# Attention keys in blocks of 128, with the last 64 of two pairs multiplied with v in the four quarters of the array

## The chip, the cores and the metric

The kernel runs on one core of one Trainium2 chip. The metric is the time on the device in microseconds, from the profiler and from repeated runs; lower is better.

## What is computed

Attention with a sigmoid in place of softmax, for 8 batches, 12 heads, 448 positions and 64 columns a head, and behind it a feed-forward layer over the 3584 tokens:

```python
scores = scale * np.matmul(q, k.transpose(0, 1, 3, 2)) - np.log(S)
attn = 1.0 / (1.0 + np.exp(-scores))
x = np.matmul(attn, v)                 # to (8 * 448, 768)
h = x @ w_in                           # (768, 2048)
g = np.maximum(0.01 * h, h)
return g @ w_out                       # (2048, 768)
```

All of it is float32.

## The kernel before

**Attention.** Two heads make a pair (48 pairs, 6 per batch): the first head's 64 columns lie in partitions 0 to 63, the second's in 64 to 127. The 448 keys are cut into NK = 4 blocks of KR = 112. For one block c, `Pair.scores` takes six matmuls into the PSUM tile `sc`, three for each head (q and k are split into a high and a low part, `qks`, and three of the four products of parts are taken), each with 64 rows, 112 weight columns and 448 streamed columns. The two heads use the two halves of the array's rows. ScalarE then writes sigmoid(scale * scores - log 448) into a tile `s` (pool `at`, five tiles). `Pair.attn_v` multiplies, for each block and head, v of that block (112 rows, 64 columns, fp32, in the halves of the array's columns) with `s`, and sums the four blocks in the PSUM tile `pv`. One slot later `Pair.keep` copies `pv` with ScalarE into a third of the tile `x`, which holds three pairs.

**FFN.** Both matmuls of the layer are taken as seven products of sums of sub-blocks (Strassen's way, in the form of Winograd) in the order `ORDER = 0, 1, 4, 5, 3, 6, 2`. Two batches (q) have four `x` tiles; `Operands` forms their sums and splits them into `so`; `PLAN` and `PLAN_ALONE` say in which slot each such step is given out: "p16": "h002" is the high part of operand 0 in the slot of product 16. `First.step` takes one product of one of NU = 8 units: nine matmuls into PSUM. A `Quad` keeps the results of a unit: product 0, 4, 3 and 2 add into one bank (`px`), product 1 and then 5 and 6 use another (`py`, `pz`). One slot after a product `Quad.done` evacuates it: 0, 4, 5 and 2 with a ScalarE copy, 1, 3 and 6 with a VectorE addition to a copy taken earlier (all of these are `c_h`).

**Order.** All instructions are kept in program order on their engines. The work is given out in slots: `slot` first issues the chores that are due and then the slot's TensorE work. For q = 0 the attention of 12 pairs runs alone. For q = 1 to 3 each pair has four attention slots (scores of blocks 0 and 1 of pair i, `attn_v` of pair i - 1 in two slots, scores of blocks 2 and 3 of pair i), followed by 5, 5 or 4 FFN products of the two batches before. The FFN of the last two batches and the second matmul come behind.

**PSUM.** In q = 0 (`ps_a`): three score tiles of two banks and two `pv`. In q = 1 to 3 (`ps_b`): two score tiles of two banks, one `pv`, two `px`, one `pz`:

```python
psum = banks("ps_b", dict(s=(2, 2), pv=(1, 1), px=(2, 1), pz=(1, 1)))
```

Beside this VectorE takes apart the weights, which come as 64-bit numbers, into float32 (`wr`, `wd`, `ws`, written to `t`), and the weights of each unit are read back and split (`wx`, `w`).

Of the kernel before, what the change touches and what calls it, by code (L numbers as in the profile page):

```python
# [9 lines left out]
F32 = mybir.dt.float32  # L10
F32R = mybir.dt.float32r
I32 = mybir.dt.int32
AF = mybir.ActivationFunctionType
# [3 lines left out]
P = 128  # L17
# [7 lines left out]
ST = 10  # L25
# [6 lines left out]
PRODUCTS = 5, 5, 4  # L32


def _f32(bits):
    return struct.unpack("<f", struct.pack("<I", bits))[0]

W_LEAST = _f32(0x38000000)  # L40
W_MOST = _f32(0x47EFFE00)


@with_exitstack
def attn_ffn_kernel(ctx: ExitStack, tc: tile.TileContext, qk, v, w_in, w_out, out):
# [6 lines left out]

    nc = tc.nc
    B = 8
    S = qk.shape[3]
    NP = qk.shape[0] // B
    D = P // 2
    KR = v.shape[1]  # L60
    NK = S // KR
    NC = out.shape[0]
    NU = w_in.shape[0]
    HW = NC // 2 * P
# [2 lines left out]
    scale = 1.0 / math.sqrt(D)  # L67
    bias = -math.log(S)
    heads = [slice(j * D, j * D + D) for j in range(2)]
# [4 lines left out]
    def pinned(issue):  # L74

        return lambda *args, **kw: tc.keep_in_program_order(issue(*args, **kw))  # L76

    mm, dma = pinned(nc.tensor.matmul), pinned(nc.sync.dma_start)
    copy, act = pinned(nc.scalar.copy), pinned(nc.scalar.activation)
# [14 lines left out]
    def later(slots, *fns, first=False):  # L94

        chores.setdefault(now + slots, ([], []))[not first].extend(fns)
# [15 lines left out]
    class Weights:  # L112


        def __init__(self, w, u, g, pool, tag, bufs=None, src=None):
            self.w, self.u, self.g, self.n = w, u, g, len(GROUPS[g])
            self.to = pool, tag, bufs
            self.src, self.stage = src, stage
# [29 lines left out]
    class Quad:  # L148
# [1 line left out]

        def __init__(self, psum, pool, tag, name, bufs, last=copy):

            self.psum, self.pool, self.tag, self.name, self.bufs = psum, pool, tag, name, bufs
            self.last = last
            self.x = self.bank("px", "px")

        def bank(self, tag, what):
            return self.psum(tag, f"{what}_{self.name}")  # L160
# [6 lines left out]
        def into(self, n):  # L167

            if n == 1:
                self.y = self.bank("pz", "py")  # L170
            elif n == 5:
                self.z = self.bank("pz", "pz")
            acc = self.y if n == 1 else self.z if n in (5, 6) else self.x
            return acc, n in (0, 1, 5)

# [20 lines left out]
    ps = ExitStack()  # L196

    def banks(name, sizes):

        pool = ps.enter_context(tc.tile_pool(name=name, bufs=1, space=PSUM, reuse_waits="tile"))  # L200

        def psum(tag, name):
            bufs, n = sizes[tag]
            return pool.tile([P, n, 512] if n > 1 else [P, 512], F32, tag=tag, name=name, bufs=bufs)

        return psum
# [4 lines left out]
    def shift(stack, name, size, side="left"):  # L211
# [5 lines left out]
    st = left.enter_context(tc.tile_pool(name="st", bufs=ST))  # L217
    warm = shift(ctx, "warm", 32, "right")
    xp, pp, raws, spl, at = (right.enter_context(tc.tile_pool(name=name, bufs=bufs, side="right")) for name, bufs in (
        ("xp", 5), ("pp", 3), ("raws", 2), ("spl", 2), ("at", 5)))  # L220
# [70 lines left out]
    class Pair:  # L291


        def __init__(self, i):
            self.i = i
            self.a = []

        def load_qk(self):
# [2 lines left out]
                dma(out=self.raw[:, x], in_=qk[self.i, :, x])  # L301

        def load_v(self):
            self.v = raws.tile([KR, 2 * NK, D], F32, tag="v", name=f"v_{self.i}", bufs=2)
            dma(out=self.v, in_=v[self.i])

        def pieces(self):

# [11 lines left out]
        def scores(self, h):  # L320
            for c in range(2 * h, 2 * h + 2):
                ps = psum("s", f"sc_{self.i}_{c}")
                for n, (kp, qp) in enumerate(((0, 0), (0, 1), (1, 0))):
                    for j, me in enumerate(heads):
                        mm(ps[:KR, j, :S], lhsT=self.parts[me, kp, 1, c * KR:(c + 1) * KR], rhs=self.parts[me, qp, 0],
                           start=n == 0, stop=n == 2)
                s = at.tile([KR, 2, S], F32, tag="s", name=f"s_{self.i}_{c}")
                act(out=s, in_=ps[:KR, :, :S], func=AF.Sigmoid, bias=bias, scale=scale)
                self.a.append(s)

        def attn_v(self, h):
            if h == 0:
                self.pv = psum("pv", f"pv_{self.i}")
            for c in range(2 * h, 2 * h + 2):
                for j, me in enumerate(heads):
                    mm(self.pv[me, :S], lhsT=self.v[:, NK * j + c, :], rhs=self.a[c][:, j], start=c == 0, stop=c == NK - 1)
            if h == 1:
                later(1, self.keep, first=True)

        def keep(self):  # L340
# [5 lines left out]
    class Operands:  # L346
# [45 lines left out]


    PLAN = {
# [19 lines left out]
    def advance(t):  # L414

        nonlocal at_load, at_high, at_low
        while at_high < len(w1) and w1[at_high][0] <= t + 3:
            w1[at_high][1].high()
            at_high += 1
        while at_low < len(w1) and w1[at_low][0] <= t + 2:  # L420
            w1[at_low][1].low()
            at_low += 1
        while at_load < len(w1) and w1[at_load][0] <= t + 8 and at_load < at_low + len(w1_stage):
            x = w1[at_load][1]
            x.stage = w1_stage[-1]
            x.load()
            at_load += 1

    class First:


# [4 lines left out]
        def step(self):  # L436
            t = (self.p + 1) * NU * NOP - len(self.todo)
            u, n = self.todo.pop(0)
            advance(t)
            p = self.p  # L440
            if n == ORDER[0]:
                self.quad = Quad(psum, st, "st", f"h{p}_{u}", ST, leaky)
                self.c = {}
            quad, c = self.quad, self.c
            w = next(x for at, x in w1[len(GROUPS) * (p * NU + u):] if n in GROUPS[x.g]).of(n)
            acc, first = quad.into(n)
            x = self.ops.t[n]
            for kk in range(NB):
                parts_mm(acc, w, slice(kk * P, kk * P + P), x[:, 0, kk], x[:, 1, kk], first and kk == 0, kk == NB - 1)
            later(1, lambda: self.after(quad, c, u, n), first=True)  # L450
# [35 lines left out]
    last = B * NP - 1  # L486
    pairs = [Pair(i) for i in range(B * NP)]
# [11 lines left out]
    first, ops = None, None  # L499
    psum = banks("ps_a", dict(s=(3, 2), pv=(2, 1)))  # L500
# [19 lines left out]
    for q in range(NQ + 1):  # L520
        before, ops = ops, Operands(q) if q < NQ else None
        if q == 0:
            slot(lambda: pairs[0].scores(0))
        elif q == 1:
            ps.close()
            psum = banks("ps_b", dict(s=(2, 2), pv=(1, 1), px=(2, 1), pz=(1, 1)))
        k = 0
        for j in range(per if q < NQ else 1):
            i = q * per + j
            if q == 0 and 0 < j:  # L530
                later(0, pairs[i + 1].load_v)
            if q == 0:
                busy = j >= per - 2
                go(q, f"e{j}.0", lambda: pairs[i].scores(1), busy)
                next_parts(i)
                if j + 1 < per:
                    go(q, f"e{j}.1", lambda: pairs[i + 1].scores(0), busy)
                    for h in range(2):
                        go(q, f"e{j}.{2 + h}", lambda: pairs[i].attn_v(h), busy)
                if j >= per - 4:  # L540
                    for t in range(2):
                        advance(2 * (j - per) + t)
                continue
            if j == 0:
                first = First(q - 1, before)
            busy = j == 0 or j == per - 1 or q == NQ
            go(q, f"e{j}.0", (lambda: pairs[i].scores(0)) if q < NQ else None, busy)
            for h in range(2):
                go(q, f"e{j}.{1 + h}", lambda: pairs[i - 1].attn_v(h), busy)
            go(q, f"e{j}.3", (lambda: pairs[i].scores(1)) if q < NQ else None, busy)  # L550
            if q < NQ:
                next_parts(i)
                if i < last:
                    later(1, pairs[i + 1].load_v)
                for _ in range(PRODUCTS[j % len(PRODUCTS)]):
                    go(q, f"p{k}", first.step, busy or j == per - 2 and k >= 50 or k < 7)
                    k += 1
# [5 lines left out]
    psum = banks("ps_f", dict(px=(3, 1), pz=(3, 1)))  # L563
# [33 lines left out]
    for k in range(NOP, NU * NOP):  # L597
        m, at = divmod(k - NOP, 6)
        if m < AHEAD:
            x = w2[use[m]]  # L600
# [22 lines left out]
    for i, (g, u) in enumerate(use[AHEAD:]):  # L623
        one = len(GROUPS[g]) == 1
        pool, tag = (ring, "ring") if i < len(GROUPS) else (t2b, "t1" if one else "t2")
        w2[g, u] = Weights(1, u, g, pool, tag, NU if one else None)
    psum = banks("ps_o", dict(px=(3, 1), pz=(5, 1)))
# [73 lines left out]
```

## Time and profile before

| | us |
|---|---|
| median of 3 runs (1118.95 to 1119.66) | 1119.5 |
| profiled execution, its own time | 1119.48 |
| its span | 1117.7 |
| TensorE busy | 1105.3 |
| VectorE busy | 651.6 |
| ScalarE busy | 618.6 |

The span is the time from the first to the last instruction that the profiler recorded. Busy times of one engine count overlapping instructions once. "PE" is TensorE's matmuls and "PEld" its weight loads, DVE is VectorE, ACT is ScalarE. Nearly all instructions carry line 76 (the helper that keeps them in order), so groups are told apart by the tiles they write and read. A matmul's duration runs from its start until its last result is out; matmuls that follow each other overlap, so the distance between starts is what one costs.

### The profile page before, as it was taken

How to read it: one execution, taken by the hardware profiler on the slowest of the kernel's cores; microseconds unless marked ns; L12 is line 12 of the kernel's file. 1: busy time of each engine (PE TensorE's matmuls, PEld its weight loads, DVE VectorE, ACT ScalarE, POOL GpSimd, SP SyncE). 2: the span in 40 equal slices, each digit the busy share in tenths (PEclk: the TensorE clock that was granted, in tenths of full speed). 3: DMA queues.
4: the chain of work that ended last, by engine and by line, in shares of the span. 5: the costliest groups of instructions: out<-in, count | busy, mean ns of one | idle time of the engine just before them, and what ended most of it. 6: DMA issues, size and time to landing. Idle time of an engine off the chain costs nothing.

```text
span 1117.7 us, 15825 instructions
## 1 busy us (share of the span) xinstructions
PE 1105.3 (99%) x5952; PEld 899.8 (81%) x5952; DVE 651.6 (58%) x886; ACT 618.6 (55%) x883; POOL 0.3 (0%) x5
## 2 busy tenths in 40 slices
PE   7999999999999999999999999999999999999998
PEld 4447777777777777777777999999999999999998
DVE  5877776777765678566648666565523333243332
ACT  6896666668666668665666655555333333323332
POOL 0000000000000000000000000000000000000000
PEclk9999999999999999999999999999999999999999
DMA  8975887975678775788654879786655555455542
GB/s 287 310 259 178 286 296 274 316 258 191 221 269 289 259 261 182 241 279 283 233 182 146 251 261 305 266 297 217 210 155 145 153 181 156 125 175 155 154 147 95
DMA packets 100828, 250.08 MB, mean 224 GB/s; under 512 B 11280, under 2 KB 51472, under 8 KB 100752
## 3 DMA queue, kind: packets, MB, share of 16 engines
q1 hardware_dynamic: 100752, 249.08, 68.2%
q8 instruction: 46, 0.75, 0.3%
q14 instruction: 30, 0.25, 0.1%
HBM read 164.63 MB, written 84.41 MB: 223 GB/s over the span
## 4 chain that ended last, share of the span: by engine, by line
PE 96%; DMA 2%; ACT 2%; DVE 0%; issue 0%; SPq 0%; ACTq 0%
PE px_o L76 21%; PE px_h L76 21%; PE pv L76 13%; PE sc L76 11%; PE pz_h L76 11%; PE pz_o L76 10%; PE py_o L76 5%; PE py_h L76 5%; DMA qk<-in_qk 1%; DMA v<-in_v 1%; ACT so L76 1%; ACT s L76 0%; ACT qks L76 0%; DVE qks L76 0%; ACT w L76 0%
## 5 line engine op out<-in xcount | busy, mean ns | idle before, releaser
L76 DVE TENSOR_TENSOR gs<-gg,gs 128x896 fp32r<-128x896 f32 x112 | 122.4, 1093 | 226.7 <-ACT gs L76 226.7
L76 PE MATMUL px_h<-so,w 128*128 128x448 f32 x1152 | 249.9, 363 | 0.2 <-ACT c_h L76 0.2
L76 PE MATMUL px_o<-gs,w 128*128 128x448 f32 x1152 | 232.5, 362 | 0.0
L76 PEld LDWEIGHTS px_h<-so,w 128*128 128x128 f32 x1152 | 214.8, 188 | 19.4 <-issue 4.5
L76 ACT CAST gs<-gg 128x896 fp32r<-128x896 f32 x112 | 105.3, 941 | 221.7 <-PE px_o L76 116.2
L76 PEld LDWEIGHTS px_o<-gs,w 128*128 128x128 f32 x1152 | 216.0, 188 | 14.4
L76 ACT ACTIVATE s<-sc 112x896 f32<-112x896 f32 x192 | 169.4, 917 | 50.2 <-PE sc L76 25.3
L76 PE MATMUL pv<-s,v 112*64 112x448 f32 x768 | 156.6, 550 | 1.0 <-DMA v<-in_v 1.0
L76 DVE TENSOR_TENSOR w<-wx,w 128x768 fp32r<-128x768 f32 (+1 forms) x160 | 136.2, 853 | 28.6 <-ACT w L76 28.1
L76 PE MATMUL sc<-qks 64*112 64x448 f32 x1152 | 143.2, 382 | 7.7 <-ACT qks L76 4.9
L76 PEld LDWEIGHTS sc<-qks 64*112 64x112 f32 x1152 | 95.5, 174 | 66.7 <-issue 34.0
L76 PE MATMUL pz_h<-so,w 128*128 128x448 f32 x576 | 128.3, 367 | 0.0
L76 ACT CAST w<-wx 128x768 fp32r<-128x768 f32 (+1 forms) x160 | 120.2, 754 | 6.2 <-DMA wx<-t 6.2
L76 PEld LDWEIGHTS pv<-s,v 112*64 112x64 f32 x768 | 51.3, 137 | 84.8 <-issue 82.4
L76 PEld LDWEIGHTS pz_h<-so,w 128*128 128x128 f32 x576 | 106.1, 187 | 14.5 <-issue 7.7
L76 PE MATMUL pz_o<-gs,w 128*128 128x448 f32 x576 | 116.5, 362 | 0.0
L76 PEld LDWEIGHTS pz_o<-gs,w 128*128 128x128 f32 x576 | 108.0, 188 | 7.2
L76 ACT COPY c_h<-px_h 128x448 f32<-128x448 f32 x64 | 34.1, 533 | 68.9 <-PE px_h L76 68.8
L76 DVE TENSOR_TENSOR qks<-qk,qks 128x896 fp32r<-128x896 f32 (+1 forms) x49 | 52.3, 1068 | 18.5 <-ACT qks L76 18.3
L76 PE MATMUL py_h<-so,w 128*128 128x448 f32 x288 | 62.8, 362 | 0.0
L76 DVE SCALAR_TENSOR_TENSOR wd<-wr,wd 128x768 int32<-128x768 int32 x64 | 61.2, 956 | 1.1
L76 ACT ACTIVATE c_h<-c_h 128x448 f32<-128x448 f32 x96 | 55.4, 577 | 10.1 <-DVE c_h L76 9.8
(37 smaller groups left out, 663.4 us busy)
## 6 DMA issues: line engine op xcount, KB each, us to landing
gg<-g SPq DMA_DIRECT2D x112, 448.0 KB, 3.5
wx<-t SPq DMA_DIRECT2D x120, 384.0 KB, 3.8
g<-c_h SPq DMA_DIRECT2D x128, 224.0 KB, 4.5
g<-s SPq DMA_DIRECT2D x96, 224.0 KB, 4.4
qk<-in_qk SPq DMA_DIRECT2D x47, 448.0 KB, 4.8
wr<-in_w_in SPq DMA_DIRECT2D x16, 768.0 KB, 7.3
t<-ws SPq DMA_DIRECT2D x16, 768.0 KB, 6.7
wr<-in_w_out SPq DMA_DIRECT2D x16, 768.0 KB, 5.9
```

The lines of the kernel that those rows point to most:

```text
L76: return lambda *args, **kw: tc.keep_in_program_order(issue(*args, **kw))
```

## The change

Pairs are put together two by two: in q = 0 the pairs 1 and 2, 3 and 4, 5 and 6, 7 and 8, in each of q = 1 to 3 the pairs 0 and 1 up to 8 and 9 of its 12 (19 twos in all). `part(i)` is 1 for the first of two, 2 for the second and 0 for a pair that stays as it was. In the first and the second the keys are cut into 128, 128, 128 and 64. The last 64 keys of the first take rows 0 to 63 of a tile `s`, those of the second rows 64 to 127 of the same tile: to get them there, the second's last block of scores is taken with 128 weight columns (keys 320 to 447), of which the upper half is used. Their product with v is taken once for both pairs, behind the second's `attn_v`, by four matmuls of 64 rows and 64 columns that use the four quarters of the array (rows by pair, columns by head). The first pair's `pv` stays open until then and is copied in the same slot as the second's. v comes in the matching layout.

For this `pv` has two banks in `ps_b`, and `px` one. The units of the first FFN matmul use the two banks `px` and `pz` in turns: even units as before, odd units with the two exchanged, so that each product writes the bank that the product before it did not. Three steps of `PLAN` move by five products, as their `x` is complete one pair later.

```diff
+JOINT_ALONE = 1, 3, 5, 7
+JOINT = 0, 2, 4, 6, 8
+PER = 12
+def part(i):
+    q, j = divmod(i, PER)
+    firsts = JOINT if q else JOINT_ALONE
+    return 1 if j in firsts else 2 if j - 1 in firsts else 0
...
-                self.y = self.bank("pz", "py")
+                self.y = self.bank(self.tags[1], "py")
             elif n == 5:
-                self.z = self.bank("pz", "pz")
+                self.z = self.bank(self.tags[1], "pz")
...
-            self.v = raws.tile([KR, 2 * NK, D], F32, tag="v", name=f"v_{self.i}", bufs=2)
-            dma(out=self.v, in_=v[self.i])
+            rows, n = ((KR, 2 * NK), (P, 2 * NK - 2), (P, 2 * NK))[self.part]
+            self.v = raws.tile([P, 2 * NK, D], F32, tag="v", name=f"v_{self.i}", bufs=2)
+            dma(out=self.v[:rows, :n], in_=v[self.i, :rows, :n])
...
-                for n, (kp, qp) in enumerate(((0, 0), (0, 1), (1, 0))):
+                if self.part == 0:
+                    k0, n, rows = c * KR, KR, slice(0, KR)
+                elif c < NK - 1:
+                    k0, n, rows = c * P, P, slice(0, P)
+                elif self.part == 1:
+                    k0, n, rows = S - D, D, slice(0, D)
+                else:
+                    k0, n, rows = S - P, P, slice(D, P)
+                for m, (kp, qp) in enumerate(((0, 0), (0, 1), (1, 0))):
                     for j, me in enumerate(heads):
-                        mm(ps[:KR, j, :S], lhsT=self.parts[me, kp, 1, c * KR:(c + 1) * KR], rhs=self.parts[me, qp, 0],
-                           start=n == 0, stop=n == 2)
-                s = at.tile([KR, 2, S], F32, tag="s", name=f"s_{self.i}_{c}")
-                act(out=s, in_=ps[:KR, :, :S], func=AF.Sigmoid, bias=bias, scale=scale)
+                        mm(ps[:n, j, :S], lhsT=self.parts[me, kp, 1, k0:k0 + n], rhs=self.parts[me, qp, 0],
+                           start=m == 0, stop=m == 2)
+                if self.part == 2 and c == NK - 1:
+                    s = pairs[self.i - 1].a[c]
+                else:
+                    s = at.tile([P, 2, S], F32, tag="s", name=f"s_{self.i}_{c}")
+                act(out=s[rows], in_=ps[rows, :, :S], func=AF.Sigmoid, bias=bias, scale=scale)
...
+            rows = slice(0, P if self.part else KR)
             for c in range(2 * h, 2 * h + 2):
+                if self.part and c == NK - 1:
+                    continue
                 for j, me in enumerate(heads):
-                    mm(self.pv[me, :S], lhsT=self.v[:, NK * j + c, :], rhs=self.a[c][:, j], start=c == 0, stop=c == NK - 1)
-            if h == 1:
+                    mm(self.pv[me, :S], lhsT=self.v[rows, (NK - 1 if self.part else NK) * j + c, :], rhs=self.a[c][rows, j],
+                       start=c == 0, stop=c == NK - 1, skip_group_check=True)
+            if h == 1 and self.part == 2:
+                x = pairs[self.i - 1]
+                for j, me in enumerate(heads):
+                    for y, rows in ((x, heads[0]), (self, heads[1])):
+                        mm(y.pv[me, :S], lhsT=self.v[rows, 2 * NK - 2 + j, :], rhs=self.a[NK - 1][rows, j],
+                           start=False, stop=True, skip_group_check=True)
+                later(1, x.keep, first=True)
+            if h == 1 and self.part != 1:
                 later(1, self.keep, first=True)
...
-        "p16": "h002", "p17": "l002", "p43": "s302", "p50": "h102", "p51": "l102 h502", "e11.0": "l502",
+        "p21": "h002", "p22": "l002", "p48": "s302", "p50": "h102", "p51": "l102 h502", "e11.0": "l502",
...
+    BANKS = ("px", "pz"), ("pz", "px")
...
-                self.quad = Quad(psum, st, "st", f"h{p}_{u}", ST, leaky)
+                self.quad = Quad(psum, st, "st", f"h{p}_{u}", ST, leaky, BANKS[u % 2])
...
-            psum = banks("ps_b", dict(s=(2, 2), pv=(1, 1), px=(2, 1), pz=(1, 1)))
+            psum = banks("ps_b", dict(s=(2, 2), pv=(2, 1), px=(1, 1), pz=(1, 1)))
```

## Rows read from the trace of the kernel before

**Rows 1.** The page, busy times: us, share of the span, instructions.

```profile
PE 1105.3 (99%) x5952; PEld 899.8 (81%) x5952; DVE 651.6 (58%) x886; ACT 618.6 (55%) x883; POOL 0.3 (0%) x5
```

**Rows 2.** TensorE's waits, whole span, all before 100 us: total, times, longest.

```profile
PE sc L76 <- ACT qks L76: 4.9, 2, 4.6
PE sc L76 <- ACT s L76: 2.1, 2, 1.8
PE pv L76 <- DMA v<-in_v: 1.0, 1, 1.0
PE sc L76 <- DVE qks L76: 0.7, 1, 0.7
PE px_h L76 <- ACT c_h L76: 0.2, 1, 0.2
```

**Rows 3.** Stretches: length, busy PE, PEld, DVE, ACT, POOL, clock, DMA share, GB/s.

```profile
23.00:79.00 56.00, 54.47 (x368) 27.53 (x364) 47.13 (x64) 48.36 (x62) 0.00 (x0) 1.00 0.88 300
...
97.00:609.00 512.00, 512.00 (x2880) 378.73 (x2881) 349.83 (x513) 338.98 (x499) 0.00 (x0) 1.00 0.75 249
...
82.00:84.00 2.00, 2.00 (x8) 0.73 (x6) 0.67 (x2) 1.85 (x3) 0.00 (x0) 0.50 0.51 201
```

**Rows 4.** TensorE's matmuls in order of time, 400 to 412 us: start, us.

```profile
399.76 1.76 PE L76 MATMUL pz_h<-so,w 128*128 128x448 f32 x8
401.36 1.97 PE L76 MATMUL px_h<-so,w 128*128 128x448 f32 x9
403.26 1.48 PE L76 MATMUL sc<-qks 64*112 64x448 f32 x12
404.67 3.23 PE L76 MATMUL pv<-s,v 112*64 112x448 f32 x16
407.83 1.47 PE L76 MATMUL sc<-qks 64*112 64x448 f32 x12
409.23 2.08 PE L76 MATMUL pz_h<-so,w 128*128 128x448 f32 x9
411.14 1.16 PE L76 MATMUL px_h<-so,w 128*128 128x448 f32 x5
```

**Rows 5.** The matmuls under way from 404.6 to 404.7 us.

```profile
404.36 0.38 PE L76 MATMUL sc<-qks 64*112 64x448 f32 x2
404.67 0.60 PE L76 MATMUL pv<-s,v 112*64 112x448 f32 x2
```

**Rows 6.** Weight loads in order of time, in narrow windows and 400 to 412 us.

```profile
403.96 0.17 PEld L76 LDWEIGHTS sc<-qks 64*112 64x112 f32 x2
...
404.17 0.17 PEld L76 LDWEIGHTS sc<-qks 64*112 64x112 f32 x2
...
405.10 0.14 PEld L76 LDWEIGHTS pv<-s,v 112*64 112x64 f32 x2 [0.23 <-issue]
405.47 0.14 PEld L76 LDWEIGHTS pv<-s,v 112*64 112x64 f32 x2 [0.23 <-issue]
...
406.98 0.14 PEld L76 LDWEIGHTS pv<-s,v 112*64 112x64 f32 x2 [0.23 <-issue]
```

**Rows 7.** ScalarE in order of time, 400 to 430 us.

```profile
407.94 0.53 ACT L76 COPY x<-pv 128x448 f32<-128x448 f32 x1 [0.52 <-PE pv L76]
408.79 1.73 ACT L76 ACTIVATE s<-sc 112x896 f32<-112x896 f32 x2 [0.31 <-PE sc L76]
```

**Rows 8.** VectorE in order of time, 400 to 430 and 190 to 196 us.

```profile
411.34 0.62 DVE L76 TENSOR_TENSOR c_h<-c_h,pz_h 128x448 f32<-128x448 f32 x1 [3.51 <-PE pz_h L76]
...
193.71 0.61 DVE L76 TENSOR_TENSOR c_h<-c_h,pz_h 128x448 f32<-128x448 f32 x1
```

**Rows 9.** TensorE's matmuls in order of time, 190 to 196 us.

```profile
192.44 3.76 PE L76 MATMUL px_h<-so,w 128*128 128x448 f32 x18
```

**Rows 10.** TensorE's matmuls in order of time, end of q = 0.

```profile
80.34 0.87 PE L76 MATMUL sc<-qks 64*112 64x448 f32 x6 [1.83 <-ACT s L76]
81.14 4.92 PE L76 MATMUL pv<-s,v 112*64 112x448 f32 x16
```

More of the change, by code (lines that the diff above doesn't have):

```diff
@@ L59, in attn_ffn_kernel @@
     D = P // 2
-    KR = v.shape[1]
-    NK = S // KR
+    NK = 4
+    KR = S // NK
     NC = out.shape[0]
@@ L148, in attn_ffn_kernel, with __init__ @@
     class Quad:
-        def __init__(self, psum, pool, tag, name, bufs, last=copy):
+        def __init__(self, psum, pool, tag, name, bufs, last=copy, tags=("px", "pz")):
             self.psum, self.pool, self.tag, self.name, self.bufs = psum, pool, tag, name, bufs
-            self.last = last
-            self.x = self.bank("px", "px")
+            self.last, self.tags = last, tags
+            self.x = self.bank(tags[0], "px")
         def bank(self, tag, what):
@@ L294, in __init__ @@
         def __init__(self, i):
-            self.i = i
+            self.i, self.part = i, part(i)
             self.a = []
@@ L684 @@
     qkd = np.stack([heads(q), heads(k)], 2)
-    vd = np.ascontiguousarray(v.reshape(B * NP, 2, NK, KR, D).transpose(0, 3, 1, 2, 4)).reshape(B * NP, KR, 2 * NK, D)
+    vp = v.reshape(B * NP, 2, S, D)
+    vd = np.zeros((B * NP, P, 2 * NK, D), np.float32)
+    for i in range(B * NP):
+        if part(i) == 0:
+            vd[i, :KR] = vp[i].reshape(2, NK, KR, D).transpose(2, 0, 1, 3).reshape(KR, 2 * NK, D)
+        else:
+            vd[i, :, :2 * NK - 2] = vp[i, :, :S - D].reshape(2, NK - 1, P, D).transpose(2, 0, 1, 3).reshape(P, 2 * NK - 2, D)
+        if part(i) == 2:
+            vd[i, :, 2 * NK - 2:] = vp[i - 1:i + 1, :, S - D:].transpose(0, 2, 1, 3).reshape(P, 2, D)
     wi = moe_w_in.reshape(2, NC // 2, P, 2, NU, P).transpose(4, 2, 0, 3, 1, 5).reshape(NU, P, 4, HW)
```

## The prediction

> **What bounds the kernel now.** I read four views, from the coarse to the fine. First the engines' busy time: TensorE is busy for 1105.3 of 1117.7 us [rows 1]. Then what TensorE itself waits for: over the whole span its five kinds of wait come to 8.9 us, the three largest of them 8.0 us, and all of it lies in the first 100 us, 0.2 us of it on an FFN product [rows 2]. So time leaves this kernel only if TensorE is given fewer steps, or if something new makes it wait. Third, its stages. In the stretch that holds three quarters of the attention (q = 1 to 3, 36 of the 48 pairs) TensorE is busy for 512.0 of 512.0 us, ScalarE for 339.0, VectorE for 349.8, at full granted clock [rows 3]. In the attention that runs alone (q = 0) TensorE is busy for 54.5 of 56 us, but ScalarE for 48.4, VectorE for 47.1, and the DMA engines 0.88 of the time: there the others are close behind [rows 3].
>
> Fourth, one pair's attention among the FFN products, matmul by matmul [rows 4]. Eight matmuls of an FFN product go from 399.76 to 401.36, 0.20 us each, so a product of 9 takes 1.80 us (409.23 to 411.14 is 1.91, as it begins with a change of shape). The pair's attention runs from 401.36 + 1.80 = 403.16 to 411.14 - 1.80 = 409.34: 6.18 us. Its score matmuls go two at a time, one per head: two start together [rows 5], and two weight loads follow every 0.20 us [rows 6], so its 24 are 12 steps, 2.40 us. Its attention-times-v matmuls are fp32 and recorded as two instructions each (16 for a pair's 8 [rows 4]); two start together [rows 5], and the next two weight loads follow 0.37 us later, and the five gaps from 405.10 to 406.98 average 0.376 [rows 6], so a block of keys is two steps of 0.375 us, 0.75 us, and the four blocks are 3.00 us. That leaves 6.18 - 5.40 = 0.78 us for four changes of the array's shape (128 rows x 128 columns, 64x128, 128x64, 64x128, 128x128), 0.195 us each on average. One can be seen alone, that into 128x64: the last scores start at 404.36, their step ends at 404.56, pv starts at 404.67 [rows 5], and its first step, to the weight loads of 405.10 [rows 6], takes 0.43 us instead of 0.375: 0.11 + 0.055 = 0.165 us. The other three share 0.615, 0.205 each.
>
> **The change, part by part.** *Blocks of 128.* Scores with 64 rows and products with 128 take the same 0.20 us step for their 448 streamed columns, so a step does not cost by its rows; three blocks of 128 cost what three of 112 cost, in scores and in pv. Weights of 128 columns are loaded in time at the 0.20 us step of the FFN products [rows 4]. Of scores there are still four blocks per pair, and sigmoids too: nothing there. The fourth pv block of both pairs goes: 2 x 0.75 = -1.50 us per two pairs.
>
> *The quarters.* Added per two pairs are four matmuls of 64 keys x 64 columns, eight instructions, on four different quarters of the array. The trace shows two column halves running together (pv) and two row halves (scores) [rows 5], never both at once. If all four quarters run together this is two steps, 0.75 us; if two at a time, 1.50; if nothing overlaps, 3.00. I take 0.75: rows show halving work in each direction, and they write two banks of PSUM, as the two row halves of the scores do. The Trainium skill ("TensorEngine Tiling (Array Packing)", Tiling Modes, Key Properties) says that different tiles can load and multiply in parallel; by it the stage is 0.75 us too, which the trace shows for two tiles only.
>
> *Two more changes of shape.* pv is followed by 64x64 quarters, and in the first of the two pairs the fourth block of scores has 64 rows x 64 columns, behind one of 64x128. Each is one change more per two pairs (the change to what follows replaces one that was there). The nearest row is the change into a 64-column shape: 0.165 each, 0.33 together. Bounds: 0, if going between these shapes costs nothing, and 0.205.
>
> *Per two pairs:* -1.50 + 0.75 + 0.33 = -0.42 us. There are 4 such in q = 0 and 5 in each of q = 1 to 3. In q = 1 to 3, where TensorE has no other wait, 15 x 0.42 = -6.3 us. In q = 0, 4 x 0.42 = 1.7 us is the most; the time per pair shrinks against a ScalarE that is busy 86% and a DMA share of 0.88 [rows 3], and one v load was already 1.0 us late [rows 2]. I take half, -0.85, bounds 0 and -1.7. The wait of 1.83 us on sigmoids at the end of q = 0, and the pv behind it that takes 4.92 us instead of 3.23, with a granted clock of 0.50 (1.2 GHz) in its middle [rows 3, 4, 10], I leave where they are.
>
> *Two keeps in one slot.* ScalarE copies both outputs after the quarters. The copy of before starts at 407.94 and occupies it until 408.47, and the next sigmoid waits for scores until 408.79 [rows 7]: 0.3 us of the second copy's 0.5 is hidden there, and what is queued behind it moves by 0.2. Those are evacuations with about a microsecond to spare (below). No cost. If nothing covered the second copy it would be 0.5 us x 15 = 7.5 us.
>
> *FFN results in two banks in turns.* This takes away a bank (px had two) and gives it to pv, which needs two live. New waits: the first product of a unit now writes the bank whose last reader is VectorE's addition for product 6 of the unit before, one product (1.80 us) earlier, and the second waits for the evacuation of product 2. For the addition in [rows 4, 8]: it ends at 411.34 + 0.62 = 411.96, the next unit starts at 411.14 + 1.80 = 412.94: 0.98 us to spare. The worst of the 32 units: the addition ends at 193.71 + 0.61 = 194.32 and the unit starts at 192.44 + 1.80 = 194.24 [rows 8, 9], 0.08 late. All other products already live with the same one-product distance, and px_h, the group with any wait on an evacuation at all, shows the one of 0.2 us [rows 2]. The operand work that moves by five products (h002, l002, s302) follows its x, which is now complete one pair later; s302 comes near the casts of the 51st product and may push an addition by some tenths in each q. I take +0.5 us for all new waits, bounds 0 and 1.5.
>
> *The rest.* v's loads are 128 rows instead of 112, at most 14% more of 48 loads; they are hidden in q = 1 to 3. The fourth block's sigmoid of the second pair writes rows 64 to 127 of the first pair's tile, which stays live for a pair longer; four of five tiles are live when the next scores begin, as before, so the second sigmoid there waits for the first pv block as it does now. Nothing.
>
> **Sum.** -6.3 - 0.85 + 0.5 = -6.65 us on the profiled execution's own 1119.5 (span 1117.7), which is the median of the runs as well: 1112.8 us.
>
> **The rivals.**
> *Quarters two at a time (slower).* The quarter stage is 1.50 us, two pairs gain -1.50 + 1.50 + 0.33 = +0.33, nineteen of them +6.3, with the waits +6.8: 1126.3 us. For it: no row shows more than two matmuls started in one step. Against it: two overlap in either direction. The stage decides at 1.50 - 0.33 = 1.17 us: above that the change loses. A harsher form: the two instructions of one matmul follow each other and starts keep their order, so that a second half blocks the next quarter; that is five steps, 1.88 us, +0.70 per two pairs, 1133.4 us. Against this form: pv would then begin with one matmul alone, and two start together [rows 5]. The Trainium skill ("TensorE: Matmul & The Clock Gate", Part 2, on LDWEIGHTS) says that matmuls stay in program order and only weight loads are pulled ahead; by that rule it would be this form. Chance of the first form 0.10, of the harsher one 0.03.
> *Changes of shape between these forms are free.* 19 x 0.75 = -14.25: 1105.2 us. For it: nothing shows a change from 128x64 to 64x64. Against: each of the four that are seen has a price. Chance 0.10.
> *Waits eat it up.* If units stall at their new bank, 6.65 us over 32 units is 0.21 us each: the additions would have to come 1.2 us later than they do. For it: one unit is late already and VectorE is busy 68% of the stretch [rows 3]. Against: 0.98 us is the usual margin. It gives 1119.5, give or take 2. Chance 0.07.
>
> **How the numbers follow.** The forecast has the remaining 0.70. Its own ends: changes of shape at 0.205 leave -0.34 per two pairs, 15 of them -5.1, nothing in q = 0, waits +1.5: 1115.9; at the other end lies the second rival, 1105.2. The range 1105.2 to 1116 holds forecast and second rival, 0.80. Less than 0.2% (2.2 us) is about what a measurement of this kernel cannot tell from no change. Faster: 0.70 + 0.10 = 0.80; same: 0.07; slower: 0.13.
>
> **What the next profile would show.** Right: 64x64 pv matmuls as a group of 152 instructions, four starting in one step of 0.375 us, about 0.9 us from the first of them to the scores behind; an attention stretch of 5.43 us where a first pair's v is multiplied (6.18 - 0.75) and of 6.51 where the quarters stand and the next first pair's scores are taken (6.18 + 0.33); px_h and pz_h still nearly without waits. Wrong: two quarters per step; a wait of TensorE on VectorE's addition at units' starts; ScalarE late with an evacuation behind two copies.

## The result and the profile after

| | before | changed |
|---|---|---|
| median, 5 runs each | 1119.39 (1118.75 to 1119.66) | 1108.24 (1107.88 to 1109.88) |
| profiled execution, its own time | 1119.48 | 1107.88 |
| its span | 1117.7 | 1106.1 |

All in us. The ratio of the runs is 0.9907 (95% interval 0.9892 to 0.9921): 11.15 us less, where 6.65 were forecast, inside the range of 1105.2 to 1116.

TensorE is still what bounds the kernel. The page's busy times (us, share, instructions) show it with 11.1 us less to do than in [rows 1], in as many instructions:

```profile
PE 1094.2 (99%) x5952; PEld 895.1 (81%) x5952; DVE 651.4 (59%) x886; ACT 617.6 (56%) x883; POOL 0.3 (0%) x5
```

What TensorE waits for in the changed kernel (total, times, longest), against [rows 2]:

```profile
PE sc L90 <- ACT qks L90: 4.6, 1, 4.6
PE sc L90 <- ACT s L90: 2.4, 2, 1.8
PE sc L90 <- DVE qks L90: 0.9, 2, 0.7
PE pv L90 <- DMA v<-in_v: 0.2, 1, 0.2
PE px_h L90 <- ACT c_h L90: 0.2, 1, 0.2
```

No wait on a bank of FFN results has come: the one of 0.2 us on `c_h` was there before, and none names an addition of VectorE. The stretch of the changed kernel with q = 1 to 3 (length, busy PE, PEld, DVE, ACT, POOL, clock, DMA share, GB/s) is again TensorE's without a gap:

```profile
97.00:604.00 507.00, 507.00 (x2891) 378.62 (x2888) 352.84 (x517) 337.92 (x501) 0.00 (x0) 1.00 0.75 252
```

Now two pairs in that stretch, TensorE's matmuls of the changed kernel in order of time (start, us). They answer to [rows 4]:

```profile
106.28 1.97 PE L90 MATMUL px_h<-so,w 128*128 128x448 f32 x9
108.17 1.49 PE L90 MATMUL sc<-qks 64*128 64x448 f32 x12
109.60 3.39 PE L90 MATMUL pv<-s,v 128*64 128x448 f32 x20
112.91 1.48 PE L90 MATMUL sc<-qks 64*128 64x448 f32 x12
114.32 2.08 PE L90 MATMUL pz_h<-so,w 128*128 128x448 f32 x9
116.24 1.96 PE L90 MATMUL px_h<-so,w 128*128 128x448 f32 x9
...
119.84 1.97 PE L90 MATMUL px_h<-so,w 128*128 128x448 f32 x9
121.74 1.48 PE L90 MATMUL sc<-qks 64*128 64x448 f32 x12
123.15 2.48 PE L90 MATMUL pv<-s,v 128*64 128x448 f32 x12
125.55 1.50 PE L90 MATMUL sc<-qks 64*128 64x448 f32 x12
...
128.89 1.96 PE L90 MATMUL py_h<-so,w 128*128 128x448 f32 x9
```

Where v of a first pair is multiplied (12 instructions), pv takes 125.55 - 123.15 = 2.40 us; before, 407.83 - 404.67 = 3.16 [rows 4]. Where the quarters are added (20 instructions), it takes 112.91 - 109.60 = 3.31. So two pairs take 5.71 us for attention times v instead of 6.32: 0.61 less (0.59 on the mean of the 15 twos, where pv of a first pair takes 2.41 us and pv of a second 3.32).

The quarters of that slot one by one (the matmuls under way in narrow windows of the changed kernel, start and us):

```profile
111.53 1.08 PE L90 MATMUL pv<-s,v 128*64 128x448 f32 x5
...
112.00 0.61 PE L90 MATMUL pv<-s,v 64*64 64x448 f32 x4
...
112.43 0.56 PE L90 MATMUL pv<-s,v 64*64 64x448 f32 x4
...
113.63 0.37 PE L90 MATMUL sc<-qks 64*64 64x448 f32 x2
113.83 0.56 PE L90 MATMUL sc<-qks 64*64 64x448 f32 x4
```

The last two halves start at 111.53. At 112.00 four quarters are under way at once, and from 112.43 the other four: the eight instructions are two steps, as forecast, and the scores follow at 112.91. The entry costs a gap of 0.47 us instead of 0.375 and a first step of 0.41 to 0.43. The narrow scores of 64x64, however, follow behind those of 64x128 at the bare step of 0.20 us (113.63, 113.83): that change of shape, which the forecast priced at 0.165, costs nothing.

The second gain lies at the end of q = 0. TensorE of the changed kernel there:

```profile
78.68 0.87 PE L90 MATMUL sc<-qks 64*128 64x448 f32 x6 [1.80 <-ACT s L90]
79.49 3.23 PE L90 MATMUL pv<-s,v 112*64 112x448 f32 x16
...
84.06 2.08 PE L90 MATMUL px_h<-so,w 128*128 128x448 f32 x9
```

The wait of 1.8 us on sigmoids is still there, but pv behind it takes 3.23 us where it took 4.92 [rows 10], and the first FFN product starts at 84.06. In the kernel before it is this row:

```profile
87.39 2.08 PE L76 MATMUL px_h<-so,w 128*128 128x448 f32 x9
```

Of these 3.33 us, 4.92 - 3.23 = 1.69 is the clock: granted at 0.50 (1.2 GHz) from 82 to 84 us in [rows 3], at 1.00 here. The other 1.64 come from the twos of q = 0 (taken apart under "q = 0 as before"). From the first FFN product to the end of the span it was 1117.7 - 87.39 = 1030.3 us and is 1106.1 - 84.06 = 1022.0: 8.3 less.

**How much of it is the change's.** The half clock behind that wait comes in some executions and not in others. Of all 13 profiles of this study, ten have a wait of 1.80 to 1.83 us there, and seven of these have a clock of 0.83 to 0.91 from 80 to 90 us; three have a wait of 0.71 to 0.89 and a clock of 1.00. A run's mean granted clock tells the two apart (0.998 or less with it, 0.999 or more without, wherever there is a profile). Compared at the same mean clock, the gain is 1119.48 - 1109.86 = 9.6 us (the profiled execution of before, and the mean of two runs of the changed kernel, at 0.998); on another chip, where both kernels have runs of both kinds, 1119.73 - 1111.04 = 8.7 at 0.998 and 1117.12 - 1108.55 = 8.6 at 1.000 (medians of 3 and 1, of 6 and 3). So some 9 us are the change's. The rest of the 11.15 is, as far as these means tell, how often the half clock happened to come.

### The profile page after: what moved, and what is told of

Read it like the earlier page. It is cut to its first block, busy times and chain, and to the rows that moved or that the text cites. A ratio compares the mean times of both kernels' runs of the same rounds, so it can differ in the third digit from the quotient of the medians.

```text
span 1106.1 us, 15810 instructions
## 1 busy us (share of the span) xinstructions
PE 1094.2 (99%) x5952; PEld 895.1 (81%) x5952; DVE 651.4 (59%) x886; ACT 617.6 (56%) x883; POOL 0.3 (0%) x5
## 4 chain that ended last, share of the span: by engine, by line
PE 95%; ACT 2%; DMA 1%; DVE 1%; issue 0%; SPq 0%; ACTq 0%
PE px_o L90 21%; PE px_h L90 21%; PE pv L90 11%; PE pz_h L90 11%; PE sc L90 11%; PE pz_o L90 10%; PE py_o L90 5%; PE py_h L90 5%; ACT s L90 1%; ACT so L90 1%; DMA v<-in_v 1%; DMA qk<-in_qk 0%; ACT qks L90 0%; DVE wd L90 0%; DVE so L90 0%
## 5 line engine op out<-in xcount | busy, mean ns | idle before, releaser
L90 ACT ACTIVATE s<-sc 128x896 f32<-128x896 f32 (+1 forms) x192 | 171.5, 917 | 59.4 <-PE sc L90 35.0
L90 PE MATMUL sc<-qks 64*128 64x448 f32 (+2 forms) x1152 | 144.7, 386 | 8.0 <-ACT qks L90 4.6
L90 PEld LDWEIGHTS sc<-qks 64*128 64x128 f32 (+2 forms) x1152 | 98.3, 180 | 65.5 <-issue 28.2
L90 PE MATMUL pv<-s,v 128*64 128x448 f32 (+2 forms) x768 | 144.1, 551 | 0.2 <-DMA v<-in_v 0.2
L90 PEld LDWEIGHTS pv<-s,v 128*64 128x64 f32 (+2 forms) x768 | 44.0, 136 | 78.3 <-issue 77.4
```

## The experiments

The theory at the start: the gain is the shared fourth block of v (two steps fewer per two pairs), the banks cost nothing, and what the forecast missed is that changes between the 64-row shapes are cheap. Ratios are to the kernel before on the same chip, each with its 95% interval.

**The banks alone.** The kernel before, with only the FFN results' two banks in turns and two banks for `pv`:

```diff
+    BANKS = ("px", "pz"), ("pz", "px")
-                self.quad = Quad(psum, st, "st", f"h{p}_{u}", ST, leaky)
+                self.quad = Quad(psum, st, "st", f"h{p}_{u}", ST, leaky, BANKS[u % 2])
-            psum = banks("ps_b", dict(s=(2, 2), pv=(1, 1), px=(2, 1), pz=(1, 1)))
+            psum = banks("ps_b", dict(s=(2, 2), pv=(2, 1), px=(1, 1), pz=(1, 1)))
```

> The kernel before with only the banks changed: px and pz in turns, two pv. Theory (new waits are covered by the 0.98 us that VectorE's addition has to spare): TensorE shows no wait behind the first 100 us, time 1119.4, at most 0.5 more. Rival (the single px makes units wait, as the prediction priced at 0.5 to 1.5 us): a TensorE wait on the addition at units' starts, 1120 to 1121.

Measured: 1119.23 us (11 runs) against 1118.66 (23 runs), ratio 1.0006 (0.9997 to 1.0015). The stretch of [rows 3] in this kernel:

```profile
97.00:609.00 512.00, 512.00 (x2881) 379.08 (x2881) 349.80 (x513) 339.14 (x500) 0.00 (x0) 1.00 0.75 249
```

TensorE is busy for all of it, as before. The banks cost nothing that shows. But this execution did not try the one unit without time to spare [rows 8, 9]. In the banks-alone kernel it is

```profile
193.38 3.76 PE L76 MATMUL px_h<-so,w 128*128 128x448 f32 x18
...
193.75 0.61 DVE L76 TENSOR_TENSOR c_h<-c_h,pz_h 128x448 f32<-128x448 f32 x1
```

On VectorE the addition stands behind work that waits for a load of weights into `wr`. In both kernels this load is given out 8.98 us ahead of the product before the unit; it landed 8.4 us later in the kernel before and 7.5 us later here. So the addition ends at 194.36 and the unit starts at 193.38 + 1.80 = 195.18, with 0.82 us to spare. The experiments with the casts come back to this unit.

**No sharing.** Blocks of 128, 128, 128 and 64 as in the change, but each of the 38 pairs multiplies its own last 64 keys with its own v:

```diff
-    return 1 if j in firsts else 2 if j - 1 in firsts else 0
+    return 3 if j in firsts or j - 1 in firsts else 0
...
                 if self.part and c == NK - 1:
-                    continue
+                    rows = slice(0, D)
```

> As changed, but each of the 38 pairs multiplies its own last 64 keys with v, two matmuls in two of the four quarters. Theory (the gain is the sharing of the quarters): a block of 64 keys costs two steps as any other, 0.75 us, and one change of shape, 0.12 to 0.16, so each of these pairs is that much slower than in the kernel before: 38 x 0.14 = +5 us, about 1124.5. Rival (the gain comes from the longer blocks or from the banks): near the changed kernel's 1108.2.

Measured: 1123.61 us, ratio 1.0046 (1.0034 to 1.0058): slower than before. One pair's pv of this kernel:

```profile
406.63 3.38 PE L90 MATMUL pv<-s,v 128*64 128x448 f32 x16
409.94 1.49 PE L90 MATMUL sc<-qks 64*112 64x448 f32 x12
```

It takes 3.31 us against 3.16: the block of 64 keys is as long as one of 112, and one more change of shape comes on top. Longer blocks by themselves bring nothing; the sharing is the whole gain.

**q = 0 as before.** The twos of q = 0 taken back:

```diff
-JOINT_ALONE = 1, 3, 5, 7
+JOINT_ALONE = ()
```

> As changed, but no twos in the attention that runs alone (q = 0), 15 twos instead of 19. Theory (each two saves 1.50 - 0.75 - 0.16 = 0.59 us wherever it stands): 4 x 0.59 = 2.4 us slower than the changed kernel, 1110.6. Rival (in q = 0 ScalarE and the DMA engines take the gain away, and what the trace shows less there is only the clock of one stage): within 1 us of the changed kernel, 1108.2 to 1109.2.

Measured: 1111.56 us, ratio 0.9931 (0.9918 to 0.9943), 3.3 above the changed kernel's median. But five of its six runs have a mean clock of 0.998; at the same clock it is 1111.67 - 1109.86 = 1.8 above, between the 2.4 of the theory and the rival's 1. The first FFN products alone cannot settle it: they start at 88.09 and 84.06, of which 1.69 us is the clock (its pv at 81.83 takes 4.92 us), but the two executions differ by 0.72 us before the first of the four twos begins. What counts is the stretch that holds the four twos, from pv of pair 1 to pv of pair 9. Its two ends in the kernel before, in this kernel and, with a wait between, in the changed one:

```profile
18.54 3.23 PE L76 MATMUL pv<-s,v 112*64 112x448 f32 x16
...
67.14 3.23 PE L76 MATMUL pv<-s,v 112*64 112x448 f32 x16
...
19.59 3.23 PE L90 MATMUL pv<-s,v 112*64 112x448 f32 x16
...
67.83 3.23 PE L90 MATMUL pv<-s,v 112*64 112x448 f32 x16
...
18.87 2.48 PE L90 MATMUL pv<-s,v 128*64 128x448 f32 x12
...
58.20 1.27 PE L90 MATMUL sc<-qks 64*112 64x448 f32 x10 [0.66 <-DVE qks L90]
...
65.48 3.23 PE L90 MATMUL pv<-s,v 112*64 112x448 f32 x16
```

It takes 48.60, 48.24 and 46.61 us: 1.6 to 2.0 less with the twos. TensorE's waits in it are 0.95, 0.63 and 1.12 us; without them 2.12 to 2.16 less, 0.53 to 0.54 per two, as in q = 1 to 3. So TensorE keeps most of the gain in q = 0 too. Some goes to waits: the 0.66 us at 58.20 and another 0.26, for the parts of q and k that VectorE splits, are in neither kernel without twos there.

**Wide halves for quarters.** The four quarters replaced by four matmuls of 64 rows and 128 columns, which use only the two row halves, so that two at a time is forced:

```diff
-                        mm(y.pv[me, :S], lhsT=self.v[rows, 2 * NK - 2 + j, :], rhs=self.a[NK - 1][rows, j],
+                        mm(y.pv[:, :S], lhsT=both[rows], rhs=self.a[NK - 1][rows, j],
```

> As changed, but the four quarters are replaced by four fp32 matmuls of 64 rows and 128 columns, in the two row halves (the weights of both heads together; this adds wrong products to the output). Only two can run at once. Theory (four quarters run at once): 4 steps instead of 2, +0.75 us for each of 19 twos, +14.3, about 1122.5. For the price of changes: if it hangs on the shape alone, the change from these halves to the scores (64 rows x 128 columns as well) is free, and the time is 19 x 0.19 = 3.6 us less, 1118.9; if it hangs on fp32 giving way to the split parts, the first scores still come some 0.1 us late and their first step takes 0.30 us.

Measured: 1120.98 us (10 runs), ratio 1.0016 (1.0008 to 1.0025). It has the four steps of the first rival. The steps, in narrow windows:

```profile
320.33 0.65 PE L90 MATMUL pv<-s,v 64*128 64x448 f32 x2
320.81 0.54 PE L90 MATMUL pv<-s,v 64*128 64x448 f32 x2
...
321.56 0.54 PE L90 MATMUL pv<-s,v 64*128 64x448 f32 x2
321.59 0.71 PE L90 MATMUL sc<-qks 64*128 64x448 f32 x2
322.14 0.77 PE L90 MATMUL sc<-qks 64*128 64x448 f32 x5
```

Four steps instead of two. The scores behind them have the same shape, 64x128, and follow without a gap: the second of their steps starts at 322.14, 0.58 behind the last wide step, 0.37 + 0.20. So here, where the shape stays, the change from fp32 to the split parts has no price of its own. Per two it is 624.36 - 615.24 over 15 (from the first product of the first FFN matmul to the first of the second): 0.61 us, which is 0.75 for two steps more, less the change behind.

**Casts later, and casts spread.** Both move operand casts of `PLAN_ALONE` from the end of q = 0 into the next products, to take away the wait of 1.80 us; the second cuts them into smaller pieces:

```diff
-        "e10.1": "s200", "e10.2": "h400 s100", "e10.3": "l400 h300", "e11.0": "l300 h600",
-        "ne0.0": "s211 h411 l600", ...
+        "e10.1": "s200", "e10.2": "h400 s100", "e10.3": "l400",
+        "ne0.0": "s211 h411", ...
```

> As changed, with the splitting of operands 3 and 6 of the first two batches moved from the end of q = 0 into the slots of the first products (whole instead of in two pieces). Theory (the 1.80 us that TensorE waits for sigmoids at the end of q = 0 is ScalarE's queue, two casts of 0.47 us of it): the wait falls to about 0.9 us, the half clock behind it does not come, and the time is 0.9 to 2.5 us less, 1106 to 1107.3. Rival (the wait is something else, or the casts only move it to the first products): a new TensorE wait on c_h behind 84 us of the same size, time unchanged.

> As changed, with the splitting of operands 3 and 6 of the first two batches in two pieces each, behind the pv of the last pair of q = 0 and in the slots of the first products. The theory of the wait at the end of q = 0 (ScalarE's queue) expects it at 0.9 us as with the whole casts later, and no wait of TensorE on an addition, as VectorE's subtraction of 1.55 us in front of it is now two of 1.09 and 0.62 at other places: 0.6 us less than with the casts whole, about 1107.0. Rival (VectorE or ScalarE is late with another evacuation there): a wait of 0.3 us or more on c_h from 84 to 95 us.

Measured: 1107.59 us, ratio 0.9901 (0.9888 to 0.9915), and 1106.88, ratio 0.9901 (0.9888 to 0.9915). The wait and what it was exchanged for, in the first of them (matmuls in time, then the load of weights and VectorE):

```profile
77.45 0.87 PE L90 MATMUL sc<-qks 64*128 64x448 f32 x6 [0.88 <-ACT s L90]
...
185.42 1.96 PE L90 MATMUL px_h<-so,w 128*128 128x448 f32 x9
187.94 2.07 PE L90 MATMUL px_h<-so,w 128*128 128x448 f32 x9 [0.55 <-DVE c_h L90]
```

```profile
177.17 0.43 SPq L90 DMA_DIRECT2D wr<-in_w_in  x1
...
185.46 0.56 DVE L90 TENSOR_SCALAR wd<-wr 128x768 int32<-128x768 int32 x1 [3.33 <-DMA wr<-in_w_in]
...
187.27 0.62 DVE L90 TENSOR_TENSOR c_h<-c_h,pz_h 128x448 f32<-128x448 f32 x1
```

0.92 us of the wait at the end of q = 0 are gone, and 0.55 come back at a bank (0.67 in the second kernel). That wait is not in the first products, where the casts now stand, but 100 us later, at the unit of [rows 8, 9]. The load of weights there is given out 185.42 - 177.17 = 8.25 us ahead of the product before the unit, as in the changed kernel (8.26), but it landed 8.3 us later and in the changed kernel 7.4. So VectorE starts on it at 185.46, the addition behind it ends at 187.89, and the unit, which could start at 185.42 + 1.80 = 187.22, starts at 187.94, 0.72 late. In the second kernel the load took 8.4 us and the unit is 0.83 late. Neither theory had this wait; the second kernel met its time all the same, and the first is 0.3 us above its range. None of the eight runs of these two has a mean clock under 0.999. Both are a little under the changed kernel (beside the second, on its chip, it ran at 1108.55, ratio 0.9917, 0.9902 to 0.9933), but their intervals overlap with its own: a better version by under 0.2%, if at all.

> The changed kernel once more, on the same chip as the other two: 1108.2 by all theories; single runs lie near 1108.0, or near 1109.8 where the pv behind the wait at the end of q = 0 runs at half clock.

**Six twos in q = 1 to 3, and both.** Also pairs 10 and 11 of each q put together, with the operand steps that need their `x` later; then the same with the later casts and a fifth two in q = 0:

```diff
-JOINT = 0, 2, 4, 6, 8
+JOINT = 0, 2, 4, 6, 8, 10
```

> As changed, with the last two pairs of each of q = 1 to 3 put together as well (18 twos there instead of 15), and the operand steps that need them later. Theory (0.59 us a two): -1.8 us, 1106.4. Rival (ScalarE now has the casts of two pairs in the first products of the next q, which then wait for their evacuations): 1108 or more, with TensorE waits on c_h at the starts of q = 2, 3 and 4.

> Six twos, casts later, and one more two in q = 0 (pairs 9 and 10). Theory: -1.8 - 0.9 - 0.6 = -3.3 us or more against the changed kernel, 1104 to 1105, with the half clock gone. Rival (the casts collect at the first products): TensorE waits on c_h there that eat 1 us or more, 1106 or more.

Measured: 1111.06 us, ratio 0.9935 (0.9923 to 0.9948), and 1109.58, ratio 0.9921 (0.9907 to 0.9934). Both slower than the change, though they have three and four twos more to gain from: from the first FFN product to the end of the span they take 1024.7 and 1024.2 us, the changed kernel 1022.0. Two lines of the first one's waits:

```profile
PE px_h L90 <- ACT c_h L90: 1.4, 4, 0.5
PE px_h L90 <- DVE w L90: 0.9, 1, 0.9
```

2.1 us more of waits than in the changed kernel. They stand among the first products behind each q (at 265.8, 438.4, 605.3 and 609.2 us), where the rival of the expectation had them, and they cost more than their own length: from start to start the products of the first FFN matmul take 415.6 us against 411.4, 4.2 more, where three twos save 1.6. Here the rival "waits eat it up" is real: the operands that need the last pairs are formed and split in the same products, and evacuations stand behind them. The last two pairs are where the margins run out.

**Quarters and one wide pass.** The change, with two more 64x128 fp32 matmuls per two behind the quarters, run once:

```diff
+                for j in range(1):
+                    for y, rows in ((x, heads[0]), (self, heads[1])):
+                        mm(y.pv[:, :S], lhsT=both[rows], rhs=self.a[NK - 1][rows, j], ...)
```

> As changed, with one more pass in the two row halves behind the quarters: two fp32 matmuls of 64 rows and 128 columns, two steps (an extra; it adds wrong products to the output). From 64 x 64 to 64 x 128 in fp32 only the width changes. Theory (a change of width alone is free, as with the scores' narrow block): two steps of 0.375 without a gap, +14.3 us, 1122.5. Rival (every change of shape in fp32 costs, and the scores' block was free because its type ignores the width): a gap of about 0.1 us and a first step longer by 0.03 to 0.05, +17 us, 1125.2.

Measured: 1123.79 us; per two 626.70 - 615.24 over 15, 0.76 us. From the quarters to the wide ones the gap is 0.465 and the first step 0.473 where 0.37 is the bare step: 0.19 us for the change. The scores behind them are free, as with the wide halves. So the same pair of shapes that costs nothing among scores (split parts, in both directions: the next run has the other one) costs 0.19 in fp32; the sum came out like the theory only because the change that followed was saved.

**The narrow scores first.** The first pair's block of 64 keys is taken ahead of its third block of 128, right behind the quarters:

```diff
-            for c in range(2 * h, 2 * h + 2):
+            for c in (NK - 1, NK - 2) if h and self.part == 1 else range(2 * h, 2 * h + 2):
```

> As changed, but the first pair of a two takes its block of 64 keys before its third block of 128, so that in q = 1 to 3 the narrow scores of the next first pair stand right behind the quarters. If a change of width is free for the split parts and only the shape 64 x 64 counts, the change from the quarters to the scores goes: the scores' first step starts 0.375 us behind the last quarters and is 0.20 long, 0.19 us less each, 2.7 us in all (14 places), 1105.5. Rival (the split parts are taken at full width whatever their columns): the gap of 0.09 us and the first step of 0.30 us stay, time unchanged.

Measured: 1107.42 us, ratio 0.9907 (0.9891 to 0.9923). The first scores behind the quarters, in narrow windows:

```profile
314.42 0.42 PE L90 MATMUL sc<-qks 64*64 64x448 f32 x2
314.68 0.57 PE L90 MATMUL sc<-qks 64*64 64x448 f32 x4
```

The last quarters start at 313.94, so the gap of 0.47 stays although the shape of 64x64 does not change, as the rival had it; the first step is 0.25 us, neither the 0.20 of the one nor the 0.30 of the other. So something is paid between the fp32 quarters and these scores, which have the same shape, and nothing between these scores and wider ones: scores of 64 columns behave here as if they were 128 wide. Why is not shown.

## Why the prediction was right, and what it sized wrongly

The mechanism was right; three sizes were off, all in one direction. At the same clock the change is worth about 9 us where 6.65 were forecast; that the measured difference is 11.15 is in part luck, the half clock.

- **-1.50 for two blocks of v, 0.75 for the quarters.** Shown. pv of a first pair lost 3.16 - 2.40 = 0.76; the quarters run four at a time in two steps. The entry into them costs 0.09 + 0.03 to 0.06, and pv of a second pair is 3.32 - 3.16 = 0.16 longer on the mean, against the 0.165 taken.
- **The mis-sized term: 0.165 for the narrow block of scores.** Measured in the steps: nothing. What all scores of q = 1 to 3 cost more is 0.7 us, 0.05 per two. So two pairs gain 0.55 instead of 0.42, and 15 of them 8.2 instead of 6.3 (8.3 measured from the first FFN product on). The forecast had taken the price of a change of shape from fp32 and used it for the split parts. The rival "changes of shape are free" was right for this one change and wrong for the entry into the quarters.
- **+0.5 for waits at the banks.** Measured: nothing in the profiles of the banks alone and of the changed kernel. The one unit that was 0.08 us late [rows 8, 9] is now just in time. The load of weights ahead of it, TensorE from the product before it on, and its addition in the changed kernel:

```profile
178.45 0.43 SPq L90 DMA_DIRECT2D wr<-in_w_in  x1
...
186.71 3.58 PE L90 MATMUL px_h<-so,w 128*128 128x448 f32 x17
...
187.70 0.62 DVE L90 TENSOR_TENSOR c_h<-c_h,pz_h 128x448 f32<-128x448 f32 x1
```

The addition ends at 188.32, and the unit starts 1.80 behind 186.71, at 188.51. That is luck in part, as the addition hangs on how long the load takes: 7.4 us here (178.45 to 185.86). Of the 12 profiles with these banks, this unit is on time in the six where the load landed within 7.4 to 7.5 us, and late in the six where it took 7.8 to 8.6: by 0.14 us (no sharing), 0.21 (six twos), 0.34 (the narrow scores first), 0.37 (q = 0 as before), 0.72 and 0.83 (the casts). So the term lies between 0 and 0.8, inside its bounds; why the load takes longer in some profiles is not shown.
- **-0.85 in q = 0.** Measured 1.6 to 2.0 in the stretch of the four twos: nearly the whole 4 x 0.54 and not half. ScalarE (busy for 86%) and a DMA share of 0.88 cost TensorE little there; the waits that came with the twos, 0.26 and 0.66 us, are on VectorE. That the half clock at the end of q = 0 would stay was the other half of this step: it comes and goes by execution, 1.69 us each time, and its absence in the profile after is not shown to be the change's doing. The 8.3 us behind the first FFN product, the 1.64 of q = 0 (with a start of the attention that differs by 0.33 us) and the clock's 1.69 make up the profiles' 11.6 us.
- **Two keeps in one slot at no cost.** Shown by ScalarE of the changed kernel: both copies as one group of 0.97 us, and the next sigmoid at 399.95, between two scores that follow without a wait of TensorE.

```profile
399.10 0.97 ACT L90 COPY x<-pv 128x448 f32<-128x448 f32 x2 [0.98 <-PE pv L90]
399.95 1.74 ACT L90 ACTIVATE s<-sc 112x896 f32<-112x896 f32 x2
```

- **The rivals.** Quarters two at a time: fell. With its two steps more per two (0.75 us) on the changed kernel's 1108.24 it would have given about 1122.5, an estimate; the wide halves have these steps and measured 1121.0, as the change behind them is saved. The 1126.3 worked out had the narrow scores' price and the waits in it. The harsher form, with five steps, fell too: four instructions start within 0.02 us of each other (112.00 to 112.02), the other four from 112.43, and no quarter is held back behind the second instruction of another quarter's matmul. The Trainium skill ("TensorE: Matmul & The Clock Gate", Part 2) says that matmuls stay in program order. The trace agrees only if the two instructions of a matmul are not neighbours in that order; its records do not name the quarter, so this stays open. The Trainium skill also says that different tiles work in parallel ("TensorEngine Tiling (Array Packing)", Tiling Modes); this trace now shows it for four.
- **Forecast stretches.** 5.43 us where a first pair's v is multiplied: from 119.84 + 1.80 to 1.80 before the product at 128.89 it is 5.45. 6.51 where the quarters stand: from 106.28 + 1.80 to 1.80 before the product at 116.24 it is 6.36; the 0.15 are the narrow scores again. Together 11.81, against 2 x 6.18 before: 0.55 less.

The 0.05 us per two that the scores cost more lie mostly in their first step behind pv, which grows with the weight columns: 0.255 us with 64 (the narrow scores first), 0.29 with 112 (before), 0.31 with 128 (changed).

What stays open: why only some executions have the half clock behind the same wait, why the load of weights takes longer in some profiles, and why scores of 64 columns cost no change of shape where fp32 matmuls of 64 columns do.

## What to carry to other kernels

Where an engine has no gap, count its steps: a block that fills half of the rows costs as many steps as one that fills them all, so two half-filled ones that meet in different quarters save a whole block. Price a change of the array's shape by number type and shape both, from the neighbours in the trace. An evacuation that stands behind a load on its engine has a margin that changes with the load: 0.8 us of landing time decided here whether TensorE waited. And before a difference of a few us is put down to a change, compare runs of the same mean clock.

## What the runs showed of the hardware

- Four fp32 matmuls of 64x64 on the four quarters of the array start within 0.02 us, the next four 0.43 us behind the first, and the scores 0.47 behind those; two steps do the eight recorded instructions.
- In fp32, going from 128x64 to 64x64 cost a gap of 0.09 us and 0.03 to 0.06 in the first step, and from 64x64 to 64x128 0.09 and 0.10. Between scores of 64x128 and 64x64, in split parts, it cost nothing (0.20 us steps throughout), and from fp32 64x128 to scores of 64x128 nothing either. From fp32 64x64 to scores of 64x64 the gap of 0.47 us stayed.
- The first step of scores behind pv took 0.255, 0.29 and 0.31 us with 64, 112 and 128 weight columns, where the later steps take 0.20.
- One and the same load of 768 KB took 7.4 to 8.6 us to land in the 13 profiles.
- After a wait of 1.80 to 1.83 us of TensorE, the granted clock fell to 0.50 in the work behind it in seven of ten profiles; after waits of 0.71 to 0.89 us in none of three.
